# Preparing a Strassen step beside the layer before it, and buffers that let a DMA queue run on

## The chip, the cores and the metric

One core of a Trainium2 chip runs the whole program. The metric is device microseconds from start to end; the profile adds one execution, recorded instruction by instruction. TensorE is called PE, VectorE DVE, ScalarE ACT, GpSimd POOL and SyncE SP. Each engine works through its own queue in order, and all DMAs around the change are issued by SP.

## The reference

```python
attn = softmax(mask(q @ k.T / 8)) @ v          # 4 batches, 8 heads, 576 positions, head size 64
                                               # heads 0-3: window 32, heads 4-7: window 128 with stride 4
x = attn as (2304, 512)
x = (sigmoid(x @ w_gate) * (x @ w_val)) @ w_out             # 512 -> 1536 -> 512
logits = x @ phi                               # 8 experts with 4 slots each: 32 slots
d = softmax over the tokens (logits);  c = softmax over the slots (logits)
slot_out[e] = relu(d[e].T @ x @ w1[e]) @ w2[e]              # e = 0 .. 7
out = c @ slot_out
```

The masks, a small constant in the denominators and reshapes are left out here.

## The kernel before

**Tiling.** The tokens come in five blocks: blocks 0 to 3 are 512 tokens of one batch each, block 4 holds the 4 x 64 that are left. A block's attention has four units, one for each pair of heads. Matmuls want about 20 bits of mantissa: an operand is split into a high part (a cast on ACT) and a low part (a subtraction on DVE or POOL), and a product is three matmuls (high x high, high x low, low x high).

**The layer `l1`.** For a block n and each of 12 column groups f of w_gate and w_val, `l1(n, f, whl, between)` runs two groups of 12 matmuls (a = 0 gate, a = 1 value), evicts them by a tanh on ACT (a = 0) and a gating product on DVE (a = 1), both at high priority, and calls `between()` after each. `split_w` makes the two halves of the weight `whl` for f (two casts on ACT, one low half on POOL, one on DVE) in one of two buffers `w`.

**Stages.** First block 0's attention, then block 0's layer with the attention of block 1 between its groups, then block 1's layer. There `between` is `beside`, called 24 times; such a call is a **tick** (tick 2f + 1 and 2f + 2 belong to f). At each tick `sab` does the next steps of the attention of blocks 2, 3 and 4, `on_tick` the steps on w_out that are due, and from tick 21 on `mix0` the first of `Post(0)`. `Post(n)` is what follows a layer: logits, softmax over tokens, transposes `tp` of the gated values into `gt`, gathers `sp` into `acc`, and `shares` (softmax over slots). Behind the layer the rest of `Post(0)` and all of `Post(1)` run. Then blocks 2 and 3 go through their layer together by Strassen's scheme with 7 products in place of 8: `pair_l1(f, ...)` for f = 0 to 11, with six matmuls for each product. Step 0 has six products, as one of each step is done in the next. Then follow block 4's layer with `Post(2)` and `Post(3)`, `Post(4)`, and the experts, whose weights (`load_e`) take whatever buffers come free (`room`, `reuse`).

**Preparing the pair.** The list `prep` holds the inputs of the first step. `pair_x2(dc)` splits block 2's activations `xf[2]` into `b_hi` and `b_lo`; `pair_sums(step)` makes four differences `tsum` on POOL, two instructions each; `pair_t(z, c)` splits them into `t_hl`; `pair_x3(c)` splits the quarter `b22` of `xf[3]`; `first_sums` and `first_splits` make the sums and the parts of the first weight (`PairW(0)`). In the kernel before, these 20 steps are spread over the steps of `Post` behind the layer, and each of their instructions is pinned (`kp`).

**Order.** A planner puts the instructions of each engine into an order ahead of time, by a model of their durations and in the order of the program where more than one is ready. `keep_in_program_order` pins an instruction behind the one that was written just before it on its engine. A buffer of a tag (`b8(tag, ...)`) is handed out when one of the tag's few buffers is free.

**Queue of SP.** Up to the end of block 1's layer (`early[0]`) the DMAs are pinned in program order through `ld`: loads of qk and v for the units, of float64 weights for `convert` (`st`), stores of converted weights (`stores`, sent by `store()` in the next `convert`), and loads of converted weights for the layer (`wst`). `convert` runs for the six slabs of w_out (z = 12 to 17) at ticks 2, 4, ... 12, and `slot_weights` transposes each three and four ticks later. The store of the last slab is sent by the `store()` behind the layer's loop.

**Attention units.** `s_step(z)` computes unit z's scores from its qk buffer (two buffers), runs `weighted(z - 2)` and `softmax(z)`, and asks for the qk load of unit z + 2. `t_step(z)` transposes the shares into a slot of `pt_ring`. A unit of blocks 0 to 3 keeps its shares in `sm4`; a unit of block 4 (z = 12 to 15) keeps them in the back of its own qk buffer:

```python
us[z]["s"] = sm4[:, HP_ORDER.index(hp)] if n < 4 else us[z]["qk"][:, 1536:2048]      # load_qk
nc.scalar.copy(pt_ring[:, u["z"] % 4]..., tr)                                        # turn_unit
```

Unit 12 has its scores in tick 10 and its transposes in tick 13.

Of the kernel before, what the change touches and what calls it, by code (L numbers as in the profile page):

```python
# [7 lines left out]
F32 = mybir.dt.float32  # L8
F32R = mybir.dt.float32r
# [8 lines left out]
P = 128  # L18
# [4 lines left out]
NF = 12  # L23
# [11 lines left out]
ND = 4  # L35
# [21 lines left out]
def tile_kernel(  # L57
# [19 lines left out]

    BUFS = {
        "xa": 2, "xb": 2, "ga": 3, "gb": 3, "w": 2, "l2": 2,
        "qk": 2, "v": 2, "bd": 1, "xt": 1, "ws": 2, "x4": 1,  # L80
    }

    def b8(tag, shape, dt, name):
# [107 lines left out]
    def turn_unit(u):  # L191
        s = u["s"].rearrange("p (c x) -> p c x", c=4)
        tr = ps_m.tile([P, 4, P], F32, tag="m", name="tr")
        for c in range(4):
            at(nc.tensor.transpose(tr[:, c], s[:, c], ident))  # L195
        nc.scalar.copy(pt_ring[:, u["z"] % 4].rearrange("p c i q -> p c (i q)"), tr)

    def weighted(u, ts, beside=None):

        n, hp = u["id"]  # L200
        dil = hp >= 2
        w = pb_tokens(n) // 4
        nq = 16 if n == 4 and dil else 32
        p_ = pt_ring[:, u["z"] % 4]
        v = u["v"].rearrange("p (t i r d) -> p t i r d", t=2, i=4, r=2)
        if "xp" not in u:
            if beside:
                u["xp"] = [x[:, 256 : 256 + 2 * w].rearrange("p (t x) -> p t x", t=2) for x in beside["bank"]]
            else:
                u["xp"] = [ps_m.tile([P, 2, w], F32, tag="m", name=f"xp{y}") for y in range(2)]  # L210
        xp = u["xp"]
        for t in ts:
            for i in range(2 if n == 4 and not dil else 4):
                for r in range(2):
                    for y in range(2):
                        o, k = xp[y][64 * r : 64 * r + 64, t], slice(64 * y, 64 * y + 64)
                        if dil:
                            o = o.rearrange("p (q f) -> p q f", f=4)[:, :, i]
                        else:
                            o = o[:, 32 * i : 32 * i + 32]  # L220
                        at(
                            nc.tensor.matmul(  # L222
                                o, lhsT=v[k, t, i, r, :], rhs=p_[k, 2 * r + t, i, 0:nq], start=True, stop=True
                            )
                        )
# [33 lines left out]
    def attn_steps(pbs, norm, head=None):  # L259
        jobs = [(n, hp) for n in pbs for hp in HP_ORDER]  # L260
        us = [{"id": j, "z": z} for z, j in enumerate(jobs)]
        tags = ["qk", "qk", "gb", "gb"] if head else ["qk"] * len(jobs)

        def load_qk(z):
            n, hp = jobs[z]
            w = 512 + k_cols(n, hp)
            us[z]["qk"] = b8(tags[z], [P, 2048], F32, "qk")
            us[z]["s"] = sm4[:, HP_ORDER.index(hp)] if n < 4 else us[z]["qk"][:, 1536:2048]
            ld(nc.sync.dma_start(us[z]["qk"][:, 0:w], qkv[n * NHP + hp, :, VCOLS : VCOLS + w]))

        def load_v(z):
            n, hp = jobs[z]
            if z % 2 == 0:
                v2 = b8("v", [P, 2, VCOLS], F32, "v2")
                us[z]["v"], us[z + 1]["v"] = v2[:, 0], v2[:, 1]
            ld(nc.sync.dma_start(us[z]["v"], qkv[n * NHP + hp, :, 0:VCOLS]))

        def load(z, what):
            if z < len(us) and not head:
                what(z)  # L280

        begun = []

        def first(what):
            if what not in begun:
                begun.append(what)
                what(0)
                what(1)

        def s_step(z, ts=range(4)):  # L290
            if z == 0 and 0 in ts:
                if head:
                    load_qk(0)
                    ld(nc.sync.dma_start(msk, masks.bitcast(BF16)))
                    load_qk(1)
                    ld(nc.sync.dma_start(cst, consts))
                    load_v(0)
                    load_qk(2)
                    load_v(1)
                    head()  # L300
                    load_qk(3)
                    load_v(2)
                    load_v(3)
                else:
                    first(load_qk)
                    first(load_v)
            scores(us[z], ts)
            if 3 not in ts:
                return
            if 2 <= z and not head:  # L310
                weighted(us[z - 2], range(2), us[z])
            softmax(us[z], norm)
            load(z + 2, load_qk)
            if z == 0:
                load(2, load_v)

        def t_step(z):
            turn_unit(us[z])

        def p_step(z, ts=range(2)):  # L320
            if head or z + 2 >= len(us):
                weighted(us[z], ts)
            if head:
                keep_warm(WP)
            if 1 in ts:
                finish_unit(us[z])
                load(z + 3, load_v)

        def sp_step(z):
            if z < len(jobs):  # L330
                s_step(z)
            if z >= 2:
                p_step(z - 2)

        steps = []
        for z in range(len(jobs) + (1 if head else 2)):
            turned = [(t_step, z - 1)] if 0 < z <= len(jobs) else []
            if head:
                score = [(s_step, z, [t]) for t in range(4)] if z < len(jobs) else []
                steps += score + turned + ([(p_step, z - 1, [t]) for t in range(2)] if z else [])  # L340
            else:
                steps += [(sp_step, z)] + turned
        return steps, lambda: first(load_qk), lambda: first(load_v)
# [56 lines left out]
    def slot_weights(f, wo_f, lag):  # L400
# [10 lines left out]
        def product():  # L411
            pt_ps = ps_m.tile([P, 2, P], F32, tag="m", name="pt_ps")
            for kc in range(ND):
                nc.tensor.matmul(
                    pt_ps[32 * kc : 32 * kc + 32], lhsT=phi[:, kc, :], rhs=wt[:, kc], start=True, stop=True
                )
            at_["pt"] = cpool.tile([P, 2, P], F32, tag="pt", name="pt")
            nc.vector.tensor_copy(at_["pt"], pt_ps)

        def summed():  # L420
# [77 lines left out]

    def pair_x2(dc):
        if dc == 0:  # L500
            pair["hi"] = b8("xb", [P, ND, 512], F32R, "b_hi")
            pair["lo"] = b8("xb", [P, ND, 512], F32R, "b_lo")
            for z, r in (("b11", slice(0, 2)), ("b21", slice(2, 4))):
                pair[z] = pair["hi"][:, r], pair["lo"][:, r]
        split(nc.vector, pair["hi"][:, dc], pair["lo"][:, dc], xf[2][:, dc])

    def pair_sums(step):
        b11, b21 = xf[2][:, 0:2], xf[2][:, 2:4]
        b12, b22 = xf[3][:, 0:2], xf[3][:, 2:4]
        if step % 2 == 0:  # L510
            pair["t", step] = b8("w", [P, 2, 2, 512], F32, "tsum")
        t = pair["t", step // 2 * 2][:, step % 2]
        one, two = {
            0: lambda: (b12, b11),
# [6 lines left out]

    def pair_x3(c):
        if c == 0:
            pair["b22t"] = b8("xa", [P, 2, 2, 512], F32R, "b22")
            pair["b22"] = pair["b22t"][:, 0], pair["b22t"][:, 1]
        hi, lo = pair["b22"]
        split(nc.vector, hi[:, c], lo[:, c], xf[3][:, 2 + c])
# [381 lines left out]
    n0 = len(after)  # L909
    mix0 = Spread(after, [(4, 12)])  # L910

    def beside():
        sab()
        on_tick()
        if ticks[0] > 20:
            mix0()

    for f in range(NF):
        whl = split_w(wst[f // 2][:, f % 2])
        if f % 2:  # L920
            load_w(f // 2 + 2)
        l1(1, f, whl, beside)
        if NF + f in wo_at:
            convert(NF + wo_at[NF + f])
    store()
    early[0] = False
    wst.clear()
    load_pair_w(0)
    load_pair_w(1)

    def first_sums():
        pair["s"] = b8("xa", [P, 2, 4, 256], F32, "s")
        prev_w[0] = PairW(0)
# [8 lines left out]
        prev_w[0].low1()  # L942
        prev_w[0].low2()

    prep = []
    for z in range(4):
        prep += [(pair_x2, z), (pair_sums, z)]
    prep += [(pair_x3, c) for c in range(2)]
    prep += [(pair_t, z, c) for z in range(4) for c in range(2)]
    prep += [(first_sums,), (first_splits,)]  # L950

    def pinned(fn, *args):
        fixed[0] = True
        fn(*args)
        fixed[0] = False

    prep = [(pinned, *x) for x in prep]
    after = after[mix0.done :] + Post(1).all()
    mix = Spread(prep, [(len(after) - 3, len(prep))])
    for fn, *args in after:  # L960
        fn(*args)
        mix()
# [15 lines left out]
    wst.clear()  # L978
    room += ["qk", "qk", "v", "v", "xb", "xa", "xa", "bd"]
    load_e(8)  # L980
    after = Post(2).all()
    n2 = len(after)
    after += Post(3).all()
# [54 lines left out]
    )  # L1038
    keep_busy(2)
    h_ps = [ps_a.tile([P, 512], F32, tag="a", name=f"h_ps{h}") for h in range(2)]  # L1040
    reuse = [None, None, "v", "v", "xb", "xa", "xa", "bd", "ga", "ga", "ga", "gb", "gb", "gb"]
    for e in range(8):
        for h in range(2):
            for kc in range(ND):
# [234 lines left out]
```

## Time and profile before

| | us |
|---|---|
| median of 3 runs (lowest, highest) | 497.81 (496.47, 498.46) |
| profiled execution | 496.94 |
| its span, first to last instruction | 495.2 |
| PE busy | 468.6 |
| DVE busy | 311.0 |
| ACT busy | 213.1 |
| POOL busy | 156.8 |

All positions below are us from the start of that span. A row of the busy times by stage gives the stage, then for each engine the us in which it was busy (and the count of instructions), the granted share of PE's clock, the DMA engines' busy share and GB/s. A matmul's duration in a row includes its run through the array, and neighbours overlap; a group's own length divided by its count is the rate.

### The profile page before, as it was taken

The numbers are of one execution on the slowest core, as the hardware profiler recorded it, in microseconds if no ns is written. First come the engines' busy times: TensorE is split into PE (matmuls) and PEld (weight loads), VectorE is DVE, ScalarE is ACT, GpSimd is POOL, SyncE is SP. The second block draws the span as 40 slices with busy tenths as digits, with TensorE's granted clock in tenths as the row PEclk, the third lists the DMA queues.
The fourth block names the chain that finished last, engine by engine and source line by source line (L and its number), as shares of the span: only waits on it lengthen the run. The fifth ranks groups of instructions, "written<-read, shape, count | busy, mean of one in ns | idle before, by whom it ended". The sixth has DMA issues, their size and how long they took to land.

```text
span 495.2 us, 12830 instructions
## 1 busy us (share of the span) xinstructions
PE 468.6 (95%) x5488; PEld 357.3 (72%) x5488; DVE 311.0 (63%) x629; ACT 213.1 (43%) x414; POOL 156.8 (32%) x132
## 2 busy tenths in 40 slices
PE   6889999999899998999889999999999999999993
PEld 3558888887788876886557888888887889742552
DVE  3879898758666745436987656655547765541532
ACT  2455645435445534314744554554535343300223
POOL 0244536416445314235154323334212124110100
PEclk9899999999999999999999999999999999999998
DMA  8979978995896079120002201201499886579997
GB/s 301 421 276 361 351 234 306 310 344 195 322 368 253 2 253 394 63 86 1 1 1 86 85 25 61 86 5 80 142 372 422 345 326 259 190 296 367 428 402 239
DMA packets 23785, 112.14 MB, mean 226 GB/s; under 512 B 2352, under 2 KB 7216, under 8 KB 14640
## 3 DMA queue, kind: packets, MB, share of 16 engines
q1 hardware_dynamic: 23408, 111.06, 60.0%
q8 instruction: 43, 0.70, 0.6%
q10 hardware_dynamic: 320, 0.26, 0.2%
q14 instruction: 14, 0.11, 0.1%
HBM read 97.16 MB, written 14.16 MB: 225 GB/s over the span
## 4 chain that ended last, share of the span: by engine, by line
PE 80%; DVE 8%; DMA 4%; ACT 2%; issue 2%; POOL 1%; SPq 1%; DVEq 0%; ACTq 0%
PE l1ps L470 32%; PE pa L592 11%; PE pe L592 6%; PE tp L757 3%; PE s_ps L222 3%; PE h_ps L1045 3%; PE lt_ps L721 3%; PE pd L592 3%; PE s_ps L162 3%; PE so_ps L1104 3%; DMA wo<-fw 2%; PE sp L786 2%; PE tr L195 2%; DMA qk<-qkv 2%; DVE s L556 1%
## 5 line engine op out<-in xcount | busy, mean ns | idle before, releaser
L470 PE MATMUL l1ps<-x_hi,whl 128*128 128x512 f32 x384 | 129.4, 402 | 2.6 <-ACT x_hi L250 2.5
L470 PEld LDWEIGHTS l1ps<-x_hi,whl 128*128 128x128 f32 x384 | 71.7, 188 | 19.0 <-ACT x_hi L250 3.2
L470 PE MATMUL l1ps<-x_lo,whl 128*128 128x512 f32 x192 | 75.6, 394 | 0.0
L382 POOL TENSOR_TENSOR fw<-fw 128x512 int32<-128x512 int32 x36 | 49.0, 1370 | 61.7 <-DVE fw L381 24.7
L470 PEld LDWEIGHTS l1ps<-x_lo,whl 128*128 128x128 f32 x192 | 36.2, 188 | 6.6 <-DVE x_lo L251 0.2
L456 DVE SCALAR_TENSOR_TENSOR g<-g,l1ps 128x512 f32<-128x512 f32 (+1 forms) x36 | 21.4, 594 | 29.3 <-PE l1ps L470 29.0
L470 PE MATMUL l1ps<-x,whl 128*128 128x256 f32 x288 | 37.0, 285 | 0.0
L470 PEld LDWEIGHTS l1ps<-x,whl 128*128 128x128 f32 x288 | 35.4, 192 | 0.4 <-issue 0.2
L480 ACT ACTIVATE g<-l1ps 128x512 f32<-128x512 f32 (+1 forms) x36 | 18.9, 526 | 37.4 <-PE l1ps L470 37.4
L434 POOL TENSOR_TENSOR whl<-w,whl 128x512 fp32r<-128x512 f32 x12 | 15.9, 1326 | 51.2 <-ACT whl L433 39.7
L379 ACT ACTIVATE fw<-st 128x512 f32<-128x512 f32 x36 | 22.8, 675 | 12.4 <-DMA st<-wd 9.2
L757 PE MATMUL tp<-cst,g 128*128 128x128 f32 x216 | 28.0, 275 | 0.0
L757 PEld LDWEIGHTS tp<-cst,g 128*128 128x128 f32 x216 | 24.0, 140 | 5.0 <-issue 3.3
L762 ACT COPY gt<-tp 128x512 f32<-128x512 f32 x27 | 15.6, 584 | 25.0 <-PE tp L757 21.9
L176 DVE TENSOR_REDUCE mx<-s_ps 128x4 f32<-128x256 f32 x40 | 15.2, 413 | 14.3 <-PE s_ps L162 8.4
L380 DVE TENSOR_SCALAR fw<-fw 128x512 uint32<-128x512 uint32 x36 | 22.7, 640 | 1.9 <-ACT fw L379 1.0
L655 DVE TENSOR_TENSOR tm<-pe,tm 128x512 f32<-128x512 f32 x12 | 8.3, 691 | 24.1 <-PE pe L592 24.1
L434 DVE TENSOR_TENSOR whl<-fw,whl 128x512 fp32r<-128x512 f32 x24 | 20.9, 884 | 3.7 <-ACT whl L433 3.2
L381 DVE TENSOR_SCALAR fw<-st 128x512 int32<-128x512 uint32 x36 | 17.8, 528 | 7.7 <-DMA wst<-wg 3.7
L189 POOL TENSOR_TENSOR sm<-sm,su 128x512 f32<-128x512 f32 x12 | 13.6, 1130 | 28.3 <-DVE su L188 26.4
L434 POOL TENSOR_TENSOR whl<-wst,whl 128x512 fp32r<-128x512 f32 x12 | 15.9, 1326 | 19.0 <-ACT whl L433 11.7
L433 ACT CAST whl<-fw 128x512 fp32r<-128x512 f32 x24 | 14.6, 620 | 16.1 <-POOL fw L382 11.7
(455 smaller groups left out, 962.1 us busy)
## 6 DMA issues: line engine op xcount, KB each, us to landing
ew<-w SPq DMA_DIRECT2D x32, 1024.0 KB, 7.8
st<-wd SPq DMA_DIRECT2D x18, 1024.0 KB, 9.1
wst<-wg SPq DMA_DIRECT2D x12, 1024.0 KB, 7.7
v<-qkv SPq DMA_DIRECT2D x20, 512.0 KB, 6.1
wg<-fw SPq DMA_DIRECT2D x12, 512.0 KB, 7.8
w<-wg SPq DMA_DIRECT2D x6, 1024.0 KB, 7.5
qk<-qkv SPq DMA_DIRECT2D x10, 576.0 KB, 5.7
qk<-qkv SPq DMA_DIRECT2D x8, 528.0 KB, 5.5
```

What stands on the lines that cost most here:

```text
L176: nc.vector.tensor_reduce(mx[:, 4 * r : 4 * r + 4], u["s_ps"][r], AX.X, ALU.max)
L379: nc.scalar.activation(top, st[:, c, 1].bitcast(F32), AF.Prelu, scale=2.0**-112, alpha=2.0**32)
L380: nc.vector.tensor_scalar(top.bitcast(U32), top.bitcast(U32), 3, None, ALU.logical_shift_left)
L381: nc.vector.tensor_scalar(low.bitcast(I32), st[:, c, 0], 2.0**-29, None, ALU.mult)
L382: nc.gpsimd.tensor_tensor(low.bitcast(I32), top.bitcast(I32), low.bitcast(I32), ALU.add)
L434: (nc.gpsimd if pool[h] else nc.vector).tensor_tensor(whl[:, 1, h], src[:, h], whl[:, 0, h].bitcast(F32), ALU.subtract)
L456: return nc.vector.scalar_tensor_tensor(g, g, 1.0, val, ALU.add, ALU.mult)
L470: nc.tensor.matmul(pt[:, 0:nt], lhsT=whl[:, w_, a, dc, :], rhs=x_[n][:, dc, :], start=first, stop=(dc == HP_ORDER[-1] and w_ == 1),)
L480: nc.scalar.activation(g, pt[:, 0:nt], AF.Tanh, scale=0.5)
L592: nc.tensor.matmul(pt, lhsT=w[:, w_, P * c : P * c + P], rhs=x_[:, c], start=first and c == 0 and w_ == 0 and x_ is hi, stop=c == 1 and w_ ...
L757: nc.tensor.transpose(tp[:, c], g_sb[self.n, 4 * q + c][:, P * j : P * j + P], ident)
L762: nc.scalar.copy(to, tp)
```

## The change

1. A unit of block 4 keeps its shares in slot 2 or 3 of `pt_ring` (2 + z % 2) and its transposed shares in slot 0 or 1.
2. `store()` is called at tick 14.
3. `prep` becomes a table of ticks: `pair_x2` at 6 to 9, `pair_sums` at 13, 14, 16 and 17, `pair_t` at 18 to 22, `first_sums` at 22, `first_splits` at 24. Only `pair_x3` stays behind the layer. The first two weight loads of the pair are issued at f = 9 and f = 11 of the layer, in SP's pinned order.
4. Buffers: `b_hi` and `b_lo` get two new ones (`bh`), `tsum` takes `l2` and `xt` in place of two `w`, `b22` takes `xb`, the small tile `pt` lies in `acc`, and the expert loads use `bh` in place of four gate buffers. The scratch for descriptors is cut to make room.

```diff
-        "qk": 2, "v": 2, "bd": 1, "xt": 1, "ws": 2, "x4": 1,
+        "qk": 2, "v": 2, "bd": 1, "xt": 1, "ws": 2, "x4": 1, "bh": 2,
...
-        nc.scalar.copy(pt_ring[:, u["z"] % 4].rearrange("p c i q -> p c (i q)"), tr)
+        nc.scalar.copy(pt_ring[:, u["slot"]].rearrange("p c i q -> p c (i q)"), tr)
...
-            us[z]["s"] = sm4[:, HP_ORDER.index(hp)] if n < 4 else us[z]["qk"][:, 1536:2048]
+            if n < 4:
+                us[z]["s"], us[z]["slot"] = sm4[:, HP_ORDER.index(hp)], z % 4
+            else:
+                us[z]["s"] = pt_ring[:, 2 + z % 2].rearrange("p c i q -> p (c i q)")
+                us[z]["slot"] = z % 2
...
-            at_["pt"] = cpool.tile([P, 2, P], F32, tag="pt", name="pt")
+            at_["pt"] = acc[:, 2, 0:256].rearrange("p (c x) -> p c x", c=2)
...
-            pair["hi"] = b8("xb", [P, ND, 512], F32R, "b_hi")
-            pair["lo"] = b8("xb", [P, ND, 512], F32R, "b_lo")
+            pair["hi"] = b8("bh", [P, ND, 512], F32R, "b_hi")
+            pair["lo"] = b8("bh", [P, ND, 512], F32R, "b_lo")
...
-            pair["t", step] = b8("w", [P, 2, 2, 512], F32, "tsum")
+            pair["t", step] = b8("l2" if step == 0 else "xt", [P, 2, 2, 512], F32, "tsum")
...
-            pair["b22t"] = b8("xa", [P, 2, 2, 512], F32R, "b22")
+            pair["b22t"] = b8("xb", [P, 2, 2, 512], F32R, "b22")
...
-    prep = []
+    prep = {}
     for z in range(4):
-        prep += [(pair_x2, z), (pair_sums, z)]
-    prep += [(pair_x3, c) for c in range(2)]
-    prep += [(pair_t, z, c) for z in range(4) for c in range(2)]
-    prep += [(first_sums,), (first_splits,)]
+        prep[6 + z] = [(pair_x2, z)]
+    for z, t in enumerate((13, 14, 16, 17)):
+        prep[t] = [(pair_sums, z)]
+    for z, t in ((0, 18), (1, 19), (2, 20), (3, 21)):
+        for c in range(2):
+            prep.setdefault(t + c, []).append((pair_t, z, c))
+    prep[22].append((first_sums,))
+    prep[24] = [(first_splits,)]
...
+    def beside():
+        sab()
+        on_tick()
+        if ticks[0] == 14:
+            store()
+        for x in prep.pop(ticks[0], ()):
+            pinned(*x)
+        if ticks[0] > 20:
+            mix0()
...
-            load_w(f // 2 + 2)
+            load_w(f // 2 + 2 if f < 9 else (f - 9) // 2)
...
-    load_pair_w(0)
-    load_pair_w(1)
...
+    late = [(pinned, pair_x3, 0), (pinned, pair_x3, 1)]
     after = after[mix0.done :] + Post(1).all()
-    mix = Spread(prep, [(len(after) - 3, len(prep))])
+    mix = Spread(late, [(2, len(late))])
...
+    room += ["bh", "bh"]
...
-    reuse = [None, None, "v", "v", "xb", "xa", "xa", "bd", "ga", "ga", "ga", "gb", "gb", "gb"]
+    reuse = [None, None, "v", "v", "xb", "xa", "xa", "bd", "bh", "bh", "ga", "ga"]
...
-    nc = bacc.Bacc("TRN2", target_bir_lowering=False, num_devices=1)
+    nc = bacc.Bacc("TRN2", target_bir_lowering=False, num_devices=1, dynamic_dma_scratch_size=256)
```

## Rows read from the trace of the kernel before

**Rows 1.** Busy times by stage; columns as told above.

```profile
111.70:226.28 114.58, 111.77 (x1813) 89.35 (x1812) 67.38 (x150) 49.52 (x99) 46.57 (x37) 1.00 0.57 208
226.28:246.10 19.82, 17.42 (x208) 11.16 (x206) 17.95 (x39) 13.21 (x28) 6.05 (x5) 1.00 0.00 1
...
226.28:266.51 40.23, 35.96 (x282) 23.54 (x280) 35.41 (x71) 22.66 (x47) 17.04 (x14) 1.00 0.08 27
200.78:226.28 25.50, 25.50 (x303) 21.44 (x303) 9.31 (x19) 7.07 (x16) 7.58 (x6) 1.00 0.12 44
```

**Rows 2.** PE's waits, 226.28 to 266.51: us in total, times, longest.

```profile
PE pa L592 <- ACT w__3519 L570: 1.2, 1, 1.2
PE sp L786 <- DVE dt L769: 0.9, 1, 0.9
PE pa L592 <- POOL w__3520 L556: 0.7, 1, 0.7
PE pe L592 <- POOL w__3519 L556: 0.6, 1, 0.6
PE lt_ps L721 <- DVE acc L794: 0.3, 1, 0.3
```

**Rows 3.** PE's waits in block 1's layer, 111.7 to 226.28.

```profile
PE wt_ps L408 <- POOL fw L382: 1.4, 1, 1.4
...
PE l1ps L470 <- POOL whl L434: 0.2, 1, 0.2
```

**Rows 4.** The chain that ended last: start us, us, what and how many.

```profile
272.25 1.36 PE pd L592 x6
...
368.25 2.76 PE lt_ps L721 x96
371.01 1.90 PE tp L757 x16
...
381.95 1.86 PE sp L786 x16
```

**Rows 5.** Groups of PE instructions, 226.28 to 266.51: busy us, mean ns.

```profile
L757 PE MATMUL tp<-cst,g 128*128 128x128 f32 x68 | 8.8, 276 | 0.0
L786 PE MATMUL sp<-gt,dt 128*32 128x512 f32 x48 | 8.1, 602 | 0.9 <-DVE dt L769 0.9
```

**Rows 6.** SP's queue in order of time: start us, us, instruction.

```profile
154.43 0.33 SPq L276 DMA_DIRECT2D v<-qkv  x1
175.37 0.33 SPq L269 DMA_DIRECT2D qk<-qkv  x1
...
177.06 0.43 SPq L365 DMA_DIRECT2D wo<-fw  x1
```

**Rows 7.** PE in order of time, block 1's layer.

```profile
174.69 0.60 PE L195 MATMUL tr<-cst,qk 128*128 128x128 f32 x4
```

**Rows 8.** DVE in order of time, with its idle time before and the releaser.

```profile
186.08 0.76 DVE L381 TENSOR_SCALAR fw<-st 128x512 int32<-128x512 uint32 x2 [1.61 <-DMA wo<-fw]
```

**Rows 9.** Groups of DVE instructions, 226.28 to 266.51.

```profile
L497 DVE TENSOR_TENSOR t_hl<-tsum,t_hl 128x512 fp32r<-128x512 f32 x8 | 5.3, 682 | 0.0
L497 DVE TENSOR_TENSOR b_lo<-xf,b_hi 128x512 fp32r<-128x512 f32 x4 | 3.3, 813 | 0.1
```

**Rows 10.** The tile whl on DVE: ns min/median/max, first and last start.

```profile
L434 DVE TENSOR_TENSOR whl<-fw,whl x24: 673/691/1787, 19.0 to 99.3; 128x512 fp32r<-128x512 f32 x24
L434 DVE TENSOR_TENSOR whl<-wst,whl x12: 632/1236/1453, 109.0 to 209.4; 128x512 fp32r<-128x512 f32 x12
```

**Rows 11.** The tile tsum on POOL; then POOL and PE in order of time.

```profile
L520 POOL TENSOR_TENSOR tsum<-xf x4: 1278/1281/1284, 218.8 to 222.5; 128x512 f32<-128x512 f32 x4
...
208.89 1.29 POOL L434 TENSOR_TENSOR whl<-wst,whl 128x512 fp32r<-128x512 f32 x1 [5.89 <-DVE g L456]
...
219.69 0.48 PE L470 MATMUL l1ps<-x_hi,whl 128*128 128x512 f32 x1
```

**Rows 12.** PE's waits from 355 to the end, the longest of six.

```profile
PE sr_ps L1122 <- ACT t L1117: 0.9, 1, 0.9
```

More of the change, by code (lines that the diff above doesn't have):

```diff
@@ L203, in weighted @@
         nq = 16 if n == 4 and dil else 32
-        p_ = pt_ring[:, u["z"] % 4]
+        p_ = pt_ring[:, u["slot"]]
         v = u["v"].rearrange("p (t i r d) -> p t i r d", t=2, i=4, r=2)
@@ L910, in tile_kernel @@
     mix0 = Spread(after, [(4, 12)])
[L912 to L920, printed above, removed]
-            load_w(f // 2 + 2)
[L922 to L927, printed above, removed]
-    load_pair_w(0)
-    load_pair_w(1)
     def first_sums():
@@ L955, in pinned @@
         fixed[0] = False
-    prep = [(pinned, *x) for x in prep]
+    def beside():
[7 more added lines that the diff above has]
+            mix0()
+    for f in range(NF):
+        whl = split_w(wst[f // 2][:, f % 2])
+        if f % 2:
+            load_w(f // 2 + 2 if f < 9 else (f - 9) // 2)
+        l1(1, f, whl, beside)
+        if NF + f in wo_at:
+            convert(NF + wo_at[NF + f])
+    store()
+    early[0] = False
+    late = [(pinned, pair_x3, 0), (pinned, pair_x3, 1)]
     after = after[mix0.done :] + Post(1).all()
-    mix = Spread(prep, [(len(after) - 3, len(prep))])
+    mix = Spread(late, [(2, len(late))])
     for fn, *args in after:
```

## Prediction, made before the changed kernel was run

> **What bounds the kernel now.** I read the busy times by stage first. From the start of block 1's layer to its last matmul (111.70 to 226.28) TensorE (PE) is busy 111.77 of 114.58 us; in the stage behind it, up to the fourth product of the second Strassen step (226.28 to 266.51), only 35.96 of 40.23 [rows 1]. In that second stage VectorE (DVE) is the full one: 17.95 of the first 19.82 us [rows 1]. So PE bounds the layer, and DVE, full of what the code calls `prep`, bounds the start of the stage behind it.
>
> Second, PE's waits. In the stage they are led by 1.2 us for ScalarE's (ACT) high parts of the first pair weight and by 0.7 and 0.6 us for GpSimd's (POOL) low parts of it; 0.9 and 0.3 us belong to the logits and gathers of block 1's `Post` [rows 2]. In the layer two matter: 1.4 us for the last conversion of a w_out slab and 0.2 us for a weight half [rows 3].
>
> Third, because a busy PE need not be PE at its rate, I priced the stage densely. Where PE runs without a gap, 16 transposes `tp` take 1.90 us (0.119 each), 16 gathers `sp` 1.86 (0.116), the 96 logit matmuls 2.76, and six Strassen matmuls 1.36 (0.227) [rows 4]. The stage holds 68 `tp` and 48 `sp` [rows 5], one set of logits, some 3 single transposes, and by the code 36 matmuls of Strassen step 0 and 30 of step 1. Dense: 68 x 0.119 + 48 x 0.116 + 2.76 + 3 x 0.119 + 66 x 0.227 = 8.08 + 5.58 + 2.76 + 0.36 + 14.96 = 31.7 us. Against 40.2 us the slack is **8.5 us**, the most the move of `prep` can bring there.
>
> **Part 1: block 4's shares leave the qk buffer.** SyncE's (SP) DMAs are pinned in order here. A `v` load starts at 154.43, and the next issue is the qk load of unit 14 at 175.37 [rows 6]. It waits for the qk buffer of unit 12, which holds that unit's shares until its transposes `tr` at 174.69 [rows 7]. Behind it SP holds a `v`, the last weight stage, a w_out store (177.06) [rows 6] and two weight loads. The last conversion needs the buffer of that store's source: DVE starts it at 186.08, released by the store's DMA [rows 8]; PE then stands 1.4 us before its transposes and 0.2 us before a weight half that ACT and POOL made behind it [rows 3]. With shares in ring slots 2 and 3, the qk buffer is free after unit 12's scores, by the code in tick 10 and not in tick 13; stage and store start with it, and the conversion ends near its own tick 12 instead of tick 16. Gain 1.4 + 0.2 = 1.6 us, of which I take **1.5**. Bounds 0 (something else late at the same place) and 1.9 (with the restart of the pipe). The slots cost nothing: slot 2 or 3 is read by the weighted sum of unit z - 2, which PE does before the softmax of unit z.
>
> **Part 2: the last w_out store at tick 14.** One SP instruction moves from behind the layer to between a `v` load and a weight load. SP waits there for POOL's sum of the last conversion; behind it are the weight loads for f = 10 and for the pair. Conversion near tick 12 means data two ticks old: 0 us. If the conversion stayed at 186 the store would hold back weights for ticks 21 on by one tick; the bound is a tick's matmuls, 12 x 0.227 = 2.7 us.
>
> **Part 3: `prep` beside the layer.** Moved out of the stage before 266.51 are, on DVE, eight `t_hl` (5.3 us), four `b_lo` (3.3) [rows 9], four half-wide sums and one low part of the first weight (by the `t_hl` row at most 5 x 0.68 = 3.4), together at most 12 us, and a cast on ACT beside most of them. The DVE then has 17.95 - 3.3 - 7 x 0.68 = 9.9 us left in the first 19.8 us, where PE has 15.9 us of dense work (all of the above but the last eight gathers and Strassen), so it stops being the bound. Where they go there is room: from tick 18 on (200.78 to 226.28) DVE is busy 9.31, ACT 7.07 and POOL 7.58 of 25.50 us [rows 1]. The eight `tsum` on POOL (1.28 us each [rows 11]) run in two bursts at the end of the layer and into the stage now; four pairs move to ticks 13, 14, 16 and 17. PE's dense rate inside the layer does not depend on them.
> What the pinned steps can hold up: on ACT the tanh of a tick and the casts of the next weight, on DVE the gating and the low half, on POOL the other low half of `whl`; PE waits for all of these. They have reach: POOL makes the low half for f = 11 at 208.89, and PE first uses f = 11 at 219.69 [rows 11]. I charge **0.3 us**; bounds 0 and 2.6 (one pair of `tsum` fully in the way once).
> DVE and POOL also slow each other. The low half on DVE takes 691 ns (median) in block 0, where no POOL twin runs, and 1236 ns in block 1, where one does [rows 10]: 0.55 us lost to a twin of about 1.28 us. Eight `tsum` then take 8 x 0.55 = 4.4 us of the 47.2 us that DVE has spare in the layer [rows 1], off the path, so nothing enters the sum. The Trainium skill (SBUF — State Buffer, section "Who interferes with whom") says it harder: a VectorE instruction with two SBUF inputs and a GpSimd one that reads SBUF exclude each other, and the later one waits in full. The row shows less than half of that; by the page each `tsum` could hold DVE for its whole length, 10.2 us over eight, and where the planner has put such an instruction ahead of a tick's gating, PE with it, so that the sum would end near +2 in place of -8.
>
> **Part 4: what is left behind the layer.** The stage keeps the `Post` work, `pair_x3` (four instructions, first needed by step 0's fifth product) and step 0. Step 0's matmuls can start with the layer's last one and fill waits; only its first three products, 18 x 0.227 = 4.1 us, can, as the next needs a buffer `l2` that block 1's gathers free. Unrelated to `prep` and still there are the 0.9 and 0.3 us [rows 2]; with restarts I leave **1.7 us** of the 8.5 standing: gain **6.8**. Bounds of what stays: 0 and 4.0 (the filler comes at the wrong place, and `Post` is a chain with gaps between gathers).
>
> **Part 5: loads and buffers later.** `bh` lets two expert loads start earlier, and two fewer wait for gate buffers in the tail. PE's waits from 355 on name no DMA [rows 12], so nothing is gained: 0 us. The smaller descriptor scratch and `pt` inside `acc` remove no instruction: 0.
>
> **Sum.** -6.8 - 1.5 + 0.3 = -8.0 us. The profiled execution took 496.94 us (span 495.2 and 1.74 around it), 0.9 under the median of 497.81, so it stands for the runs: 488.9 by it, **489.8** by the median.
>
> **Rivals.**
> (a) *Only the recorded waits on `prep` go.* The planner orders PE's queue ahead, and if step 0 stays behind Post's chain, the stage loses 1.2 + 0.7 + 0.6 = 2.5 us [rows 2] and the conversion its 1.5: 493.8. For it: the limit of 18 filler matmuls. Against it: DVE at 91% of the stage's first half [rows 1] slows even the matmuls counted as busy.
> (b) *The work moves and the time with it.* The layer grows by what the stage loses, because evictions come behind pinned casts. About 497.8. Against it: from 200.78 on DVE would be busy (9.31 + 5.3 + 3.4) / 25.50 = 71% [rows 1, 9].
> (c) *Slower: POOL's `tsum` in the path.* POOL runs in order; if the planner puts each pair of `tsum` ahead of the low half that PE needs next, PE waits 2 x 1.28 at each of four ticks, 10.2 us, against 8.3 gained: 499.7. It decides from the point where POOL's lead falls under 2.6 us; it is 10.8 us at f = 11 [rows 11], but it was gone at f = 8, where the 0.2 us wait names this very instruction [rows 3]. The same price comes about on DVE if each `tsum` there holds up an instruction ahead of a gating for its full 1.28 us. That is the rule of the Trainium skill cited in part 3 (SBUF — State Buffer).
> (d) *It doesn't do what it says*: a buffer that is not yet free (`xt` at tick 16, freed by the store of tick 14) holds the third `tsum`, and with it all pinned steps, so `prep` ends behind the layer again. Then only part 1 is left: 496.3.
>
> **How the numbers follow.** Forecast 0.58, (a) 0.20, (b) 0.05, (c) 0.11, (d) 0.06. A measurement of this kernel can tell about 0.5%, or 2.5 us, from no change. Faster takes the forecast and (a): 0.78; same takes (b) and (d): 0.11; slower (c): 0.11. The range begins at 497.8 - 8.5 - 1.9 - some 0.9 for a lower base, 486.5, and reaches to the upper bounds, 497.8 - 4.5 - 1.3 + 2.6 = 494.6, which takes (a) in and leaves (b), (c) and (d) out.
>
> **What would show it.** Right: no SP gap between 155 and 175, the last conversion before tick 14, `t_hl` and `tsum` all before the layer's last matmul, and some 33 us instead of 40.2 from there to the same product. The layer should last about 113 us. Wrong: l1 matmuls waiting for POOL `whl` or for ACT and DVE behind a cast (c, b); first Strassen matmuls no earlier than 15 us after the layer (a); `tsum` behind the layer (d).

## The result, and the profile after

The changed kernel takes 490.03 us (median of 4 runs, 488.91 to 491.67); the kernel before, on the same chip, 497.61 (496.47 to 498.46). The ratio is 0.9838 with an interval of 0.9804 to 0.9873, so about 7.6 to 7.8 us less. The profiled execution was the slowest of the four, 491.67 us with a span of 489.9.

Busy times of the changed kernel by stage, columns as in [rows 1]: the layer (first to last matmul of block 1's `l1`), the first 19.82 us behind it, the whole stage up to the same product as before, and the last 25.5 us of the layer.

```profile
113.46:226.74 113.28, 111.32 (x1811) 89.17 (x1809) 75.72 (x166) 57.42 (x114) 54.00 (x44) 1.00 0.59 209
226.74:246.56 19.82, 19.72 (x225) 13.20 (x224) 16.19 (x36) 7.47 (x16) 2.31 (x2) 1.00 0.29 107
226.74:259.68 32.94, 32.84 (x283) 24.05 (x281) 26.26 (x55) 15.09 (x30) 7.93 (x8) 1.00 0.27 97
201.24:226.74 25.50, 24.86 (x270) 20.51 (x269) 15.45 (x30) 12.32 (x27) 5.91 (x7) 1.00 0.12 43
```

The **stage** takes 32.94 us against 40.23 [rows 1], and PE is busy in all but 0.10 of it. The **layer**, counted for both kernels from its own first matmul (112.04 before; [rows 1] begin with the transposes ahead of it), takes 113.28 us against 114.24. PE's waits from 113 to 260, which answer to [rows 2, 3], have shrunk to two lines:

```profile
PE s_ps L222 <- issue: 1.3, 2, 1.1
PE wp_ps L427 <- DVE x L251: 0.6, 1, 0.6
```

The first was there before (1.3 us, one wait); it varies from 0.3 to 1.5 us between executions of all kernels here. The second is new. All the waits of [rows 2] are gone, those on `Post` included.

By the two profiled executions the difference is only 5.3 us: layer -1.0, stage -7.3, but +1.4 in the 113 us ahead of the layer and +1.5 behind the stage. Neither is shown to come from the change. In the twelve profiled executions told of here the layer starts between 111.17 and 113.46 us (111.17 in experiment 10, whose kernel is the changed one but for the ticks of a few steps), and the stretch behind the stage is 228.4 to 229.0 us long in seven of them and 229.9 to 230.2 in five, where PE's clock falls (last section). So I compare layer and stage by the traces, and whole times by the medians.

SP's queue of the changed kernel, as in [rows 6] (start, us, instruction):

```profile
156.01 0.33 SPq L280 DMA_DIRECT2D v<-qkv  x1
161.39 0.33 SPq L273 DMA_DIRECT2D qk<-qkv  x1
...
162.29 1.46 SPq L365 DMA_DIRECT2D st<-wd  x1
163.84 0.38 SPq L369 DMA_DIRECT2D wo<-fw  x1
...
174.50 0.49 SPq L280 DMA_DIRECT2D v<-qkv  x1
179.33 0.33 SPq L369 DMA_DIRECT2D wo<-fw  x1
```

The qk load of unit 14 goes out at 161.39 (175.37 before), and stage and store follow at once. The last store of w_out is at 179.33. POOL in order of time, with the last conversion and the `tsum`:

```profile
178.01 1.29 POOL L386 TENSOR_TENSOR fw<-fw 128x512 int32<-128x512 int32 x1 [0.78 <-DVE fw L385]
...
187.84 2.53 POOL L524 TENSOR_TENSOR tsum<-xf 128x512 f32<-128x512 f32 x2
...
197.61 5.03 POOL L524 TENSOR_TENSOR tsum<-xf,tsum 128x512 f32<-128x512 f32 x4
202.59 1.73 POOL L438 TENSOR_TENSOR whl<-wst,whl 128x512 fp32r<-128x512 f32 x1
```

All eight `tsum` (2.51 us for the first pair at 169.93) and all `t_hl` (204.26 to 219.72 on DVE) lie in the layer. How the stage changed is seen on PE and DVE. Before, in order of time, gathers `sp` stand in small groups between Strassen's first matmuls, and on DVE the copies to `gt` that they need stand between the splits of `prep`:

```profile
243.84 1.06 PE L786 MATMUL sp<-gt,dt 128*32 128x512 f32 x6
246.10 0.50 PE L592 MATMUL pa<-b_hi,w__3519 128*128 128x512 f32 x1 [1.20 <-ACT w__3519 L570]
...
247.34 1.05 PE L786 MATMUL sp<-gt,dt 128*32 128x512 f32 x4
248.62 0.73 PE L592 MATMUL pe<-t_hl,w__3519 128*128 128x512 f32 x2 [0.23 <-ACT w__3519 L572]
249.29 1.05 PE L786 MATMUL sp<-gt,dt 128*32 128x512 f32 x4
...
245.92 0.68 DVE L497 TENSOR_TENSOR t_hl<-tsum,t_hl 128x512 fp32r<-128x512 f32 x1
246.52 0.68 DVE L760 COPY gt<-tp 128x512 f32<-128x512 f32 x1
247.12 0.68 DVE L497 TENSOR_TENSOR t_hl<-tsum,t_hl 128x512 fp32r<-128x512 f32 x1
...
248.05 0.68 DVE L760 COPY gt<-tp 128x512 f32<-128x512 f32 x1
```

PE had ended its last transposes at 243.9; DVE copies the last two results 2.6 and 4.2 us later. After, DVE copies two of them at once, `Post` runs through and Strassen follows:

```profile
242.56 1.92 PE L790 MATMUL sp<-gt,dt 128*32 128x512 f32 x16
244.58 0.48 PE L596 MATMUL pa<-b_hi,w__3241 128*128 128x512 f32 x1
...
242.02 1.28 DVE L764 COPY gt<-tp 128x512 f32<-128x512 f32 x2
```

The 16 gathers in a row take 1.92 us; the two groups of four before took 1.05 us each.

### The profile page after: what moved, and what is told of

Same layout as the page of the kernel before. It is cut to its first block, busy times and chain, and to the rows that moved or that the text cites. A ratio compares the mean times of both kernels' runs of the same rounds, so it can differ in the third digit from the quotient of the medians.

```text
span 489.9 us, 12823 instructions
## 1 busy us (share of the span) xinstructions
PE 467.3 (95%) x5483; PEld 359.4 (73%) x5488; DVE 309.0 (63%) x629; ACT 214.8 (44%) x414; POOL 155.0 (32%) x132
## 4 chain that ended last, share of the span: by engine, by line
PE 89%; DVE 3%; ACT 2%; issue 1%; DMA 1%; POOL 1%; SPq 0%; DVEq 0%; ACTq 0%; POOLq 0%
PE l1ps L474 33%; PE pa L596 13%; PE pe L596 6%; PE tp L761 4%; PE so_ps L1113 3%; PE pd L596 3%; PE s_ps L222 3%; PE h_ps L1054 3%; PE sp L790 3%; PE s_ps L162 3%; PE lt_ps L725 3%; PE tr L195 2%; DMA qk<-qkv 1%; PE wt_ps L412 1%; PE op L1152 1%
## 5 line engine op out<-in xcount | busy, mean ns | idle before, releaser
L383 ACT ACTIVATE fw<-st 128x512 f32<-128x512 f32 x36 | 22.9, 677 | 10.2 <-DMA st<-wd 10.2
L766 ACT COPY gt<-tp 128x512 f32<-128x512 f32 x27 | 15.8, 585 | 25.9 <-PE tp L761 21.7
L162 PE MATMUL s_ps<-qk 64*32 64x64 f32 x1280 | 17.7, 228 | 3.3 <-issue 2.2
```

What stands on the lines that cost most here:

```text
L162: nc.tensor.matmul(u["s_ps"][r][32 * i : 32 * i + 32, t, :], lhsT=q[64 * r : 64 * r + 64, 128 * t + 32 * i : 128 * t + 32 * i + 32], rhs=k ...
L383: nc.scalar.activation(top, st[:, c, 1].bitcast(F32), AF.Prelu, scale=2.0**-112, alpha=2.0**32)
L766: nc.scalar.copy(to, tp)
```

## Experiments

The stage repeats well: the changed kernel and three kernels that leave it untouched had 32.94, 32.95, 32.91 and 32.95 us. So a difference of a few tenths there, read from one profiled execution, counts. The layer is given with the wait for `issue` taken off, at which no edit aims: 112.94 us before, 111.98 after. Each edit also lets the planner order the engines anew, so an experiment shows what its load and the new order do together.

**1. Slots and early store alone.** The kernel before with the block 4 lines of the diff and `if ticks[0] == 14: store()`.

> The kernel before, with block 4's shares in the ring slots and the last w_out store at tick 14, and nothing else. Theory (the two parts add up): the SP queue runs on at tick 10, PE's 1.4 us wait for the last conversion and 0.2 us for the weight half go, the layer of block 1 lasts 113.0 us in place of 114.58, and the stage behind it stays at 40.2: about 496 us, 1.5 below the kernel before. Rival (the parts need each other): the work that the early conversion frees is not used as long as the preparation is behind the layer, and the time stays within 0.5 us of 497.6.

Measured: 496.15 us (495.22 to 500.14), ratio 0.998 (0.9951 to 1.0008). Layer 111.92, 111.5 without `issue`; stage 40.18.

```profile
PE wp_ps L427 <- DVE x L251: 0.5, 1, 0.5
PE s_ps L222 <- issue: 0.4, 1, 0.4
```

The 1.4 us for the conversion and the 0.2 us for the weight half [rows 3] are gone from the layer, and the wait for `x` has come with the slots, with no `prep` in the layer. Net, the layer is 1.4 us shorter; the ratio puts it at 1.0, and no change at all lies inside its interval.

**2. Everything but the slots.** The changed kernel with the shares of block 4 in the qk buffer again:

```diff
-                us[z]["s"] = pt_ring[:, 2 + z % 2].rearrange("p c i q -> p (c i q)")
+            us[z]["s"] = sm4[:, HP_ORDER.index(hp)] if n < 4 else us[z]["qk"][:, 1536:2048]
```

> The changed kernel with block 4's shares in the qk buffer again. Theory: the preparation keeps its ticks, the stage behind the layer stays at 33 us, and the layer gains a wait of 1.4 to 1.6 us for the last conversion: 491.5 against 490.0. Rival (the buffer xt): the last conversion, its transposes and its store come three ticks later, the third tsum waits for them on POOL, with it the pinned splits and the low halves of the weights behind it, and the time rises by 4 us or more.

Measured: 493.46 us (491.73 to 495.97), ratio 0.9909 (0.9881 to 0.9938). Stage 32.95 as after. Layer 117.30, of which `issue` 0.3: 5.0 us longer than after on this count. Its longest wait, then SP, POOL and DVE around it:

```profile
PE wt_ps L408 <- POOL fw L382: 3.2, 1, 3.2
```

```profile
154.67 0.33 SPq L276 DMA_DIRECT2D v<-qkv  x1
175.59 0.33 SPq L269 DMA_DIRECT2D qk<-qkv  x1
```

```profile
185.92 2.72 POOL L520 TENSOR_TENSOR tsum<-xf 128x512 f32<-128x512 f32 x2
189.66 2.60 POOL L382 TENSOR_TENSOR fw<-fw 128x512 int32<-128x512 int32 x2 [1.03 <-DVE fw L380]
...
186.48 2.44 DVE L381 TENSOR_SCALAR fw<-st 128x512 int32<-128x512 uint32 x2 [1.79 <-DMA wo<-fw]
```

SP stalls from 155 to 175 as before, the last conversion is late again, and now it meets a pair of `tsum`: DVE's two steps of it take 2.44 us beside them against 0.76 for the same two [rows 8], and POOL's sums come after. PE waits 3.2 us where it waited 1.4. In this wait PE's granted clock falls to its lower level, 1.2 GHz, and stays there until about 196.8:

```profile
190.00:195.00 5.00, 3.91 (x15) 3.13 (x16) 0.69 (x1) 2.24 (x4) 3.78 (x4) 0.50 1.00 374
195.00:200.00 5.00, 5.00 (x141) 4.19 (x141) 2.67 (x5) 1.10 (x2) 0.99 (x1) 0.82 0.76 263
```

So the 5.0 us are two things: 2.6 us more of waits (3.2 in place of 0.6), and 2.5 us by which PE is busy longer in the layer (113.83 against 111.32). The medians put the slots at 3.4 us here; whether the clock falls in every execution of this kernel is not known. Either way the slots are worth more with `prep` in the layer than the 1.4 us that they are worth alone: the two parts are not independent. Neither expectation is met.

**3. Everything but `prep`.** The changed kernel with all 20 steps of `prep` spread over `Post` behind the layer, as before; slots, store, loads and buffers as after (`tsum` in `w`).

> The changed kernel with the preparation behind the layer again (and tsum on the two w buffers again); the early store, the shares in the ring, the early weight loads of the pair and the new buffers stay. Theory: the stage goes back to about 40 us and the layer to 113.0 us, as the 0.6 us wait behind tsum goes: 496 us. Rival (the buffers made the difference, above all the pair's weights, which wait at SP, and the separate buffers for b_hi and b_lo): the stage stays under 36 us, 492 us or less.

Measured: 495.43 us (493.24 to 498.99), ratio 0.9954 (0.9927 to 0.9981). Layer 112.42, 111.6 without `issue`. The stage:

```profile
224.68:263.95 39.27, 35.28 (x282) 23.35 (x280) 35.02 (x71) 22.72 (x47) 17.09 (x14) 1.00 0.24 81
```

Moving `prep` alone thus takes 39.27 - 32.94 = 6.3 us from the stage and puts some 0.4 into the layer; by the ratios (0.9954 and 0.9838) it is worth 5.8 us. The rest of the stage, 40.23 to 39.27, is not `prep`.

**4. Buffers of the pair.** The kernel of experiment 3 with `b_hi` and `b_lo` in `xb` and `b22` in `xa`:

```diff
-            pair["hi"] = b8("bh", [P, ND, 512], F32R, "b_hi")
+            pair["hi"] = b8("xb", [P, ND, 512], F32R, "b_hi")
```

> The kernel with all preparation behind the layer (slots, early store, loads and all other buffers as in the changed one), with b_hi and b_lo in the layer's xb buffers and b22 in xa again, as in the kernel before. It asks where the 0.9 us of the stage comes from by which that kernel (39.27 us) is shorter than the slots alone (40.18 us). Theory (the buffers: casts and subtractions that need not wait for the layer's own tiles let the planner order the stage otherwise): stage 40.2 us again, 496. Rival (the earlier pair loads, or another order that has nothing to do with buffers): stage 39.3 us, 495.4, as there.

Measured: 496.01 us (493.69 to 497.82), ratio 0.9964 (0.9932 to 0.9995). The stage is back at its old length:

```profile
225.36:265.59 40.23, 35.91 (x283) 23.54 (x281) 35.45 (x71) 22.69 (x47) 17.03 (x14) 1.00 0.08 27
```

So 0.9 us come from the buffers (the times alone could not tell the two kernels apart); the earlier pair loads, which this kernel keeps, are worth nothing here. The `b_lo` run at the same place in both, the first 3.8 us behind the layer, but the low parts of `b22` do not. First experiment 3, with `b22` in `xb`, then this kernel, with `b22` in `xa`:

```profile
233.08 0.67 DVE L501 TENSOR_TENSOR b<-xf,b 128x512 fp32r<-128x512 f32 x1
...
241.20 1.29 DVE L501 TENSOR_TENSOR b<-xf,b 128x512 fp32r<-128x512 f32 x2
```

They run from 8.4 us behind the layer there and from 15.8 us here, among the last copies of `Post`, and the first weight's cast on ACT begins 1.0 us later (19.1 against 18.2 us behind the layer). So the buffer of `b22` is the likely source of the 0.9 us; it was not changed by itself.

**5. Load on DVE without dependencies.** The changed kernel with twelve subtractions of one quarter repeated on DVE behind the layer, the same values again:

```diff
+    def again(c):
+        hi, lo = pair["b22"]
+        kp(nc.vector.tensor_tensor(lo[:, c], xf[3][:, 2 + c], hi[:, c].bitcast(F32), ALU.subtract))
+    late += [(pinned, again, z % 2) for z in range(12)]
```

> The changed kernel with 12 subtractions of 128x512 on DVE (0.68 us each, 8.2 us) put among the steps behind the layer: they repeat the low half of b22 with the same result, and no Post step needs them. It is the DVE work that the change took away, without its waits for buffers and weights. Theory (DVE's load bounds the stage): DVE has 26.3 us to do in 32.9 now and 34.4 then, most of it in the first 20 us, so the stage grows by 4 to 7 us: 494 to 497. Rival (the chain of the preparation bounded it: splits, sums, w buffers, first weight): the stage grows by less than 1.5 us, 491.5 at most.

Measured: 491.96 us (489.56 to 495.04), ratio 0.9891 (0.9852 to 0.993). Layer 113.45; the stage:

```profile
225.82:261.53 35.71, 34.64 (x282) 23.53 (x280) 33.01 (x67) 14.91 (x31) 8.85 (x8) 1.00 0.25 89
```

2.8 us of the 6.3 come back, and only 0.9 of them are recorded as waits: a load that nothing waits for makes PE "busy" 1.8 us longer for the same matmuls. The planner orders PE otherwise, too: Strassen's first matmul now stands at 240.33, ahead of the last 24 gathers, of which two groups of four take 1.05 us each. Both expectations missed, and more than the load is needed to explain experiment 3.

**6. The same load on ACT.** Twelve casts, `nc.scalar.copy(hi[:, c], xf[3][:, 2 + c])`, at the same places.

> The changed kernel with twelve casts to the high part of one quarter repeated on ACT behind the layer (12 x 0.62 = 7.4 us, the same values again, nothing waits for them), at the same places where the run with the repeated subtractions has its twelve on DVE. Theory (what counts in the stage is that DVE is full; ACT is busy 15.09 of 32.94 us there and has room): stage 32.9 to 33.6 us, 490 to 490.7. Rival (any pinned work there stands in the way of evictions, on whichever engine): stage 35 to 36 us as with the subtractions on DVE, 492 to 493.

Measured: 489.95 us (489.3 to 495.25), ratio 0.9885 (0.9811 to 0.9958), too wide to tell. The stage, and PE where it is lost:

```profile
225.26:259.86 34.60, 34.47 (x282) 24.15 (x281) 26.73 (x55) 21.02 (x42) 7.89 (x8) 1.00 0.26 92
...
243.26 0.50 PE L596 MATMUL pa<-b_hi,w__3241 128*128 128x512 f32 x1
...
244.04 1.04 PE L790 MATMUL sp<-gt,dt 128*32 128x512 f32 x2
```

34.60 us lies between the two expectations. ACT had room on average, and still 1.4 of the 1.7 us are lost at one place, around the last two gathers, which stand between Strassen's first matmuls and take 1.0 us; the trace records no wait. An engine's mean share does not say that pinned work on it is free.

**7. The first weight late.** The changed kernel with `first_sums` and `first_splits` behind the layer, the splits near the end of `Post`.

> The changed kernel with the first pair weight's sums and splits (some 2 to 3 us on DVE, as much on ACT and POOL) behind the layer again, the splits at the end of Post as before; the tsum, t_hl and b_lo stay in the layer. Theory (most of the 7.3 us of the stage is the chain weight sums, splits, first product, behind the last Post step): stage 36 to 38 us, PE waits for w behind ACT and POOL of 2 to 3 us in sum as in the kernel before, layer 0 to 0.5 us shorter, 492.5 to 494.5. Rival (the load on DVE is what counts, and of it this is a quarter): stage 33.5 to 34.5 us, 490.3 to 491.3.

Measured: 490.29 us (489.32 to 491.65), ratio 0.9834 (0.9794 to 0.9875). Layer 113.02 (111.9 without `issue`), stage 225.67 to 259.82, 34.15 us: +1.2, as the rival (load) had it. Late splits of the first weight are not most of the gain; that theory falls. The chain is tried only in part: DVE makes the sums at 228.5 to 231.4 here, and made them at 247.7 to 250.3 in the kernel before.

**8. Both.** The loads of experiment 5 and the first weight of experiment 7 together.

> The changed kernel with both: twelve low-part subtractions of one quarter repeated on DVE behind the layer (8.2 us in which nothing waits for them), and the first weight's sums and splits behind the layer again. Theory (load and chain together are the whole of what preparing beside the layer saves in the stage): stage 38 to 40 us, as with all of the preparation behind the layer (39.3), 494.5 to 496. Rival (a third part is the t_hl themselves, for which the fifth product and those behind it wait): stage 35.5 to 37.5 us, 492 to 494.

Measured: 493.86 us (492.62 to 496.59), ratio 0.9921 (0.9897 to 0.9945). Layer 112.77. The stage, and PE's longest waits in it:

```profile
225.95:264.10 38.15, 34.62 (x283) 23.69 (x281) 35.19 (x71) 17.04 (x35) 10.48 (x10) 1.00 0.24 84
```

```profile
PE sp L790 <- DVE gt L764: 1.2, 1, 1.2
PE sp L790 <- DVE dt L773: 0.8, 1, 0.8
```

+5.2 us, more than 2.8 + 1.2, with DVE as full as before (35.19 us). The waits show that a full DVE delays the gathers of `Post`. It delays the weight as well: the sums stand behind the twelve subtractions here (245.8 to 249.0), so this is not quite the sum of the two edits, and on top of the load the late weight costs 2.4 us (38.15 - 35.71) in place of 1.2. The 1.1 us up to experiment 3 is left for the rest of `prep`, the `t_hl` among it.

**9. POOL doubled.** The changed kernel with each `tsum` done twice.

```diff
+            for _ in range(2):
-            kp(nc.gpsimd.tensor_tensor(t[:, c], one[:, c], two[:, c], ALU.subtract))
+                kp(nc.gpsimd.tensor_tensor(t[:, c], one[:, c], two[:, c], ALU.subtract))
```

> The changed kernel with each of the eight tsum on POOL done twice in a row (the second writes the same values again): 8 x 1.28 = 10.2 us more on POOL in the layer, nothing else. Theory (POOL has a lead over PE, and only the tsum of ticks 16 and 17, which run in one stretch of 5.03 us at 197.6, have used it up): the layer grows by about 5 us at this one place, to some 118 us, in one wait for wp_ps behind the POOL whl that follows; the pairs of ticks 13 and 14 cost nothing; the stage stays at 33 us; 494 to 496. Rival (c) of the prediction, now doubled (each pair stands in PE's path): PE waits 2.6 us at each of the four places, layer about 123 us, 499 to 501. Rival (POOL is not in the path at all, and the 0.6 us wait is DVE's own): layer within 1 us of 113.3.

Measured: 490.42 us (489.01 to 490.62), ratio 0.9829 (0.9792 to 0.9866). Layer 113.28 (112.6 without `issue`), POOL in order of time, and two of PE's waits:

```profile
112.38:225.66 113.28, 111.47 (x1810) 89.04 (x1809) 79.82 (x166) 56.98 (x114) 66.75 (x52) 1.00 0.59 209
...
186.21 5.69 POOL L525 TENSOR_TENSOR tsum<-xf 128x512 f32<-128x512 f32 x4
...
195.60 11.55 POOL L525 TENSOR_TENSOR tsum<-xf,tsum 128x512 f32<-128x512 f32 x8
207.12 3.44 POOL L438 TENSOR_TENSOR whl<-wst,whl 128x512 fp32r<-128x512 f32 x2
```

```profile
PE wp_ps L427 <- DVE x L251: 0.6, 1, 0.6
PE l1ps L474 <- POOL whl L438: 0.6, 1, 0.6
```

10.2 us more on POOL (12.8 by its busy time) cost 0.6 us, at the one stretch of 11.55 us. My 5 us and rival (c)'s 10 both miss; the third expectation, a layer within 1 us, holds. The wait for `x` is the same as without doubling, so I had wrongly taken it for POOL's and for a lead used up (experiment 1, without `prep` in the layer, has it at 0.5 us).

**10. The pairs of `tsum` apart.** `pair_sums` at 13, 14, 16, 18 and the second and third sums' splits swapped.

> The changed kernel with the fourth pair of tsum one tick later (18 in place of 17) and the second and third sums' splits t_hl swapped, so that no two pairs of tsum run in one stretch. Theory (the one PE wait that is left in the layer, 0.6 us for wp_ps at 203.5, comes from POOL's stretch of 5.03 us): this wait goes, layer 112.6 to 112.9 us, stage unchanged at 33 us, 489.3 to 489.7, which the times alone cannot tell from the changed kernel. Rival (the planner gathers the pairs again, or the wait moves to the next tick): a wait of 0.4 to 1 us between 200 and 212, layer as in the changed kernel, 490.0.

Measured: 489.55 us (486.81 to 491.01), ratio 0.9837 (0.9794 to 0.988). The wait for `x` stays at 0.6 us, and the last four `tsum` still run back to back (194.4 to 198.1). So the rival's planner holds, and the theory falls. The layer lasts 112.35 us, 111.65 without `issue`, 0.3 less than in the changed kernel; the first `tsum` already runs 1.0 us earlier behind the layer's start (55.5 us against 56.5), ahead of the edit, 0.6 of it by `issue`. No kernel here is faster than the changed one by more than the runs can tell.

## Why the prediction held, step by step

**The sum** was -8.0, the medians give -7.6 to -7.8, stage and layer by the traces -8.3. It held term by term in the large ones, and one of the small ones hid a mistake. The range's upper end took 1.3 us for part 1, whose own lower bound was 0; with 0 it would be 495.9, which changes nothing here.

**Part 4, the stage: -6.8 predicted, -7.3 measured.** The dense price of 31.7 us was the right floor: the stage came down to 32.94, so 1.2 us stay standing, not 1.7. Of the 7.3, the move of `prep` makes 6.3 (experiment 3) and the buffers 0.9 (experiment 4), which **part 5** had put at 0: it looked for a transfer that PE waits for, and what they changed, as far as the rows show, is where the splits of `b22` run. Rival (a) fails here, and one sees why: of the 7.3 us, 4.2 were idle time of PE (40.23 - 35.96, less the 0.10 left), and 3.1 lay in PE's busy time (35.96 against 32.84 for the same matmuls). The waits that (a) counted were 2.5 us, all of [rows 2] 3.7, about half of the gain; the dense price put its bound at 8.5. DVE's load by itself brings back 2.8 us, the first weight's place 1.2, both 5.2, each with a new order of PE, which no run parts from the load.

Two steps on the way were wrong. I said that Strassen's matmuls would *fill* the waits of `Post`, and named a first one no earlier than 15 us behind the layer as the sign for (a). The first came at 244.58, 17.8 us behind the layer, and yet the whole gain was there: with the splits gone from between DVE's copies, `Post` ran densely by itself and there was nothing to fill. And DVE was to have 9.9 us left in the first 19.8 us; it had 16.19. The stretch is equal in time, not in work: the stage ran faster, so more of `Post`'s own evictions fell into it (eight copies to `gt` in place of six, six sums into `acc` in place of four); and one low part of the first weight, which I had moved out, still ran there (1.37 us at 227.61). Over the whole stage DVE's work did drop, from 35.41 to 26.26 us, 9.2 of the "at most 12" that I moved.

**Part 1: -1.5 predicted, -1.4 measured** by the layer of experiment 1. But the pieces differ: 1.6 us of waits went and a new one of 0.5 us came, behind the old ones in time (203 against 186). The stall of SP shrank from 20.9 to 5.4 us. The last conversion was not done near tick 12 but at 179.3, in tick 13 to 14: its stage goes out at 162.29 and takes about 9 us to land.
The sum treated part 1 as separate from `prep`. Experiment 2 shows that it is not: without the slots, `prep` in the layer costs 117.0 - 112.94 = 4.1 us, of which 2.4 are PE's longer busy time at the fallen clock; with them it costs 0.4. The prediction's terms were right only because the change makes both.

**Part 2: 0 predicted, 0 measured, for another reason.** The store waits: SP is free at 175 and issues it at 179.33, 0.03 us after POOL ends the last conversion (178.01 + 1.29). The data were not two ticks old. It costs nothing because behind it stand only the weight loads for f = 10 and for the pair, issued from 179.75 on, and the first of them is split on ACT at 200.47.

**Part 3: +0.3 predicted, +0.4 measured** (111.98 against 111.62 in experiment 3, both without `issue`). The five kernels with the slots and untouched `tsum` in the layer (the changed one, experiments 5 to 8) have 111.9 to 112.1, the three with the slots and `prep` behind the layer (1, 3 and 4) 111.5 to 111.8; experiment 10, with another order of the `tsum`, has 111.65. Rival (b) falls with it: in the layer's last 25.5 us DVE is busy 15.45, 6.1 more than before, and 61% where (b) feared 71. Rival (c) put the decision at POOL's lead, 10.8 us at f = 11 [rows 11]: that lead was about the right number, and the fear that it is gone at f = 8 was not, since that wait came from the conversion and left with it. In the changed kernel POOL has the low half for f = 10 done at 204.3, behind its stretch of 5.03 us, and PE first needs it at 210.1, 5.8 us later; the doubled stretch is 6.5 us longer, and PE waits 0.6.
On contention, eight more `tsum` brought DVE's busy time in the layer to 79.82 us. The same 166 instructions took 75.72 us in the changed kernel and 76.9 to 77.2 in experiments 5, 6 and 10, so 0.3 to 0.5 us went for each, under the 0.55 taken from [rows 10]. The Trainium skill (SBUF — State Buffer, section "Who interferes with whom") has the later of two such instructions wait in full; by it up to 1.28 us would have been lost for each. What is measured is a quarter to two fifths of that, over all the instructions that happened to stand beside a `tsum`, so it need not contradict the rule for a single meeting; how much of a `tsum`'s length met such an instruction, no run shows.

**Rival (d)** falls: `xt` was free in time and the third pair ran at 197.61. Of `prep` in the layer only the last low parts of the first weight ran on behind its last matmul, to 228.98 on DVE; PE uses that weight from 244.58.

## What to carry over

Price a stage densely, from places where the same instructions run without a gap, and take the slack from that: PE's busy time can hold nearly as much lost time as its recorded waits. Two edits that each look independent may share a queue; ask of each what it costs without the other. When a stretch of equal length is compared before and after, compare the work in it too. And look at the clock of a stretch before its length is called the effect of an edit.

## What the runs showed of the hardware

In the profiled execution of the changed kernel PE's granted clock fell for some 4 us in the tail, to 0.56 and 0.59 of full speed, near its lower level of 1.2 GHz; just ahead PE had been busy 1.73 of 2.00 us. Busy times, columns as above, and PE in order of time:

```profile
430.00:432.00 2.00, 1.73 (x15) 1.29 (x15) 0.56 (x1) 0.00 (x0) 0.00 (x0) 1.00 0.93 356
432.00:434.00 2.00, 2.00 (x12) 0.59 (x16) 0.00 (x0) 0.00 (x0) 0.00 (x0) 0.56 0.34 143
434.00:436.00 2.00, 2.00 (x16) 0.44 (x8) 0.00 (x0) 0.00 (x0) 0.00 (x0) 0.59 0.51 143
...
432.00 4.48 PE L1033 MATMUL si_ps<-wos,fin 128*32 128x512 f32 x24 [0.22 <-DVE fin L1028]
```

The same 24 matmuls in the kernel before:

```profile
438.94 2.78 PE L1024 MATMUL si_ps<-wos,fin 128*32 128x512 f32 x24 [0.22 <-DVE fin L1019]
```

These 1.7 us account for the 1.5 by which the stretch behind the stage is longer in this execution, and they would pass for a loss of the change if one compared the two profiles alone. The same fall stands at this place in five of the twelve profiled executions: those of the changed kernel and of experiments 2, 7, 8 and 9. All five have `prep` in the layer, as three of the seven others have; whether the change makes the fall likelier is open. In the head, between 24 and 36 us, the granted clock was 0.86 in this execution and 1.00 in the one before; between 12 and 24 us it was 0.86 in both.

The other fall, in experiment 2, came at 190 while PE stood idle (187.9 to 191.1); with it PE's busy time in that layer is 2.5 us longer.
